# Output projection of a linear-attention block: the order of 1/den loads, x rows, first FFN weights and PQ products

## Chip, cores and metric

One core of a Trainium2 chip runs the whole kernel in one launch. The metric is the device time in microseconds (us), the median over several runs; lower is better. The kernel before takes 782.52 us (three runs, 782.25 to 782.95).

## What is computed

An adaLN-conditioned transformer block over 2048 tokens of width 1024: linear attention with 32 heads of width 32, then a GEGLU feed-forward network (FFN) of width 3584. All inputs are bf16.

```python
mod = (silu(c) @ w_mod)                 # six rows of 1024: sa, ca, ga, sb, cb, gb
h = layernorm(x) * (1 + ca) + sa
q, k, v = split(h @ wqkv)               # 32 heads
pq, pk = phi(q), phi(k)                 # where(t > 0, t + 1, exp(t)) + 1e-6
kv = einsum('bhsd,bhse->bhde', pk, v);  z = sum_s pk
num = pq @ kv;  den = pq . z + 1e-6
x = x + ga * ((num / den) @ wo)
h = layernorm(x) * (1 + cb) + sb
x = x + gb * ((gelu(h @ w_gate) * (h @ w_up)) @ w_down)
```

## The kernel before

The tokens are cut into 16 chunks of 128, and the chunks into 4 groups of 512 (`sg` 0 to 3), each group into two halves of 256 tokens (`h` 0 and 1). Five instruction streams run side by side, one for each engine: PE (TensorE), DVE (VectorE), ACT (ScalarE), POOL (GpSimd) and SP, which issues nearly all DMAs. Every operation is recorded by `sch.op` or `sch.dma` with the bytes it reads and writes; `Sched` works out the semaphore waits from them. Within one engine, work runs in the order of its stream. SP has eight semaphore lanes in turn, so each DMA also waits for the landing of the eighth one before it (`Sched.LANES`, `dma`).

The order of the streams: PE's and SP's are those of the program text. DVE, ACT and POOL are put in a new order by `sch.reorder` from the K/Q stage up to the point `mark[1]`, just before the projection's loop over chunks 3 to 13; there a planner with costs and due times picks the next ready operation. `deps=` adds an order by hand: an operation with it waits for the one named. Behind `mark[1]` DVE's order is again that of the text, so what stands in the table `SLOT` comes in the order written.

The stages around the change:

- **M and KV.** `m_tile(g, k, ...)` makes M = pk^T x for eight blocks `g` of 128 head columns, three column tiles `k` each: 24 tiles, in the list `tiles`, with matmuls at L895. ACT copies each tile to the buffer `mb` (L900). When a block is done, `m_t(g)` transposes it by a DMA from `mb` to `mtb` (L703); "mT7" below is that of the last block. `kv_prod(g, ...)` (L913) multiplies it by the V weights, and DVE masks the result into `kvt` (L920). `w2_pair(i)` (L1201) multiplies two blocks of `kvt` by the output weights to W2, which ACT or DVE copies from PSUM (L1208).
- **1/den.** `den(pr_, b)` computes the denominators of two groups (L1240), DVE takes the reciprocal (L1245, L1246), and a DMA stores it in DRAM (L1248). `rb_load(sg, hs)` loads it back for one half of a group, spread over the partitions: four DMAs of 256 KB for each half (L1260). There are two buffers, `RB[0]` for even groups and `RB[1]` for odd ones.
- **PQ products.** `pq_scale(sg, h, gs)` multiplies pq in place by 1/den on DVE (L1273), four operations for each half of a group.
- **Projection.** `wo_mm(c, b0, gs)` accumulates pq @ W2 for chunk `c` in PSUM banks `b0` and `b0 + 1` (L1283); after the last block DVE adds x and the row sum (L1291, "x1"). Chunks 0 to 2 are interleaved with the last KV and W2 products; chunks 3 to 13 follow whole, with `SLOT[c]()` behind each; chunks 14 and 15 stand within the first FFN unit. The banks go round, so chunk 4 needs those of chunk 0.
- **LN2 and FFN.** For each chunk POOL and ACT compute the second layernorm (L664 to L679, L674, L660), and a DMA transposes the rows (`h2a`, `h2b`, L703). `x_dma(c0, c1)` loads rows of x again (L592); chunks 7 and up had been overwritten before. `wt_dma(u)` loads the gate and up weights of FFN unit `u` (two DMAs of 512 KB, L1371); DVE and ACT form sums of them for the products (`t_sum`, L1433).

The table `HOOK` says what stands behind which of the 24 M tiles. Its end, before:

```python
19: "kv4", 20: "den1 ps0.0", 21: "gbr", 22: "ps0.1", 23: "rb2.0"}
```

Here `rb2.0` is `rb_load(2, (0,))` and `ps0.1` is `pq_scale(0, 1, ...)`. In the loop over tiles, `m_t(g)` of tile 23 comes ahead of the hooks of tile 23, so mT7 stands on SP ahead of `rb2.0`.

Of the kernel before, what the change touches and what calls it, by code (L numbers as in the profile page):

```python
# [7 lines left out]
ACTF = mybir.ActivationFunctionType  # L8
# [322 lines left out]
def bass_adaLN_cond__linear_attn_block__geglu_ffn__prompt_kernel(  # L331
# [18 lines left out]
    with ExitStack() as es:  # L350
# [150 lines left out]
        def r_wt(i, t0=0, t1=2, k0=0, k1=NDC):  # L501
            return [(OFF_WS + i * 8192 + t * 4096 + k0 * 512, OFF_WS + i * 8192 + t * 4096 + k1 * 512, f"wt{i}") for t in range(t0, t1)]
# [28 lines left out]
        def r_rb(i, h, g0=0, g1=NG):  # L531
            return [(OFF_RB[i] + (h * NG + g0) * 1024, OFF_RB[i] + (h * NG + g1) * 1024, f"rb{i}")]
# [58 lines left out]
        def x_dma(c0, c1):  # L591
            return sch.dma(Q, lambda e: e.dma_start(XALL[:, c0:c1, :], x_v[:, c0:c1, :]), wr=r_xs(c0, c1), note=f"x{c0}")  # L592
# [312 lines left out]
        def m_t(g):  # L905
            i = g % 2
            tdma(Q, MTB[i][:, :, :], MB[g][:, :], r_mb(g), r_mtb(i), f"mT{g}")

        def kv_prod(g, bank):
            i = g % 2  # L910
            o = None
            for dc in range(NDC):
                o = sch.op(T, lambda e, dc=dc: e.matmul(PS(bank, 0, P), WV[:, g, dc, :], MTB[i][:, dc, :],  # L913
                                                        start=(dc == 0), stop=(dc == NDC - 1)),
                           rd=r_wv(g) + r_mtb(i), pwr=(pr(bank) if dc == 0 else ()), note=f"kv g{g} dc{dc}")
            pset_writer(bank, o)
            z = 64 * (g % 2)
            for h in range(2):
                a, gz = 64 * h, g // 2 * 2 + h
                sch.op(V, lambda e, a=a, gz=gz: e.tensor_tensor(KVT[z:z + 64, gz, 0:64], ps_all[a:a + 64, bank * 512 + a:bank * 512 + a + 64], BMASK[a:a + 64, a:a + 64], ALU.mult),  # L920
                       prd=pr(bank), rd=r_sm("bmask"), wr=r_kvt(gz, gz + 1), note=f"kvt{g}", overwrite_ok=True)

        bank_i = [0, 4]
# [268 lines left out]
        def z32():  # L1192
            sch.op(V, lambda e: e.tensor_tensor(Z32[:], BM32[:], ZCOLS[:, :].unsqueeze(2).to_broadcast([P, NG, NH]), ALU.mult),
                   rd=r_sm("bm32") + r_sm("zcols"), wr=r_sm("z32"), note="z32")

        def w2_pair(i, b0=4):
            for hf in range(2):
                for r in range(2):
                    for h in range(2):
                        b, g = b0 + 2 * r + hf, 2 * i + h  # L1200
                        sch.op(T, lambda e, b=b, g=g, h=h, r=r, hf=hf: e.matmul(ps_all[64 * h:64 * h + 64, b * 512:(b + 1) * 512], KVT[64 * r:64 * r + 64, g, 0:64],  # L1201
                               WO[64 * r:64 * r + 64, g, hf * 512:(hf + 1) * 512], start=True, stop=True),
                               rd=r_kvt(g, g + 1) + r_wo(g, hf * 512, (hf + 1) * 512), pwr=pr(b), note=f"w2 {i}.{hf}", overwrite_ok=True)
            for r in range(2):
                b, g = b0 + 2 * r, 2 * i + r
                w_, p_ = W2[:, g, :], ps_all[:, b * 512:(b + 2) * 512]
                eng = V if i > 1 and r else A
                sch.op(eng, lambda e, w_=w_, p_=p_, eng=eng: e.activation(w_, p_, ACTF.Copy) if eng == A else e.tensor_copy(w_, p_),  # L1208
                       prd=pr(b) + pr(b + 1), wr=r_w(OFF_WK, "w2", g), note=f"w2cp{g}")

        def wofold(kc):
# [53 lines left out]

        GH = [((0, 2), (2, 4)), ((4, 6), (6, 8))]

        def pq_scale(sg, h, gs):
            i, t0 = sg % 2, h * HW
            for g0, g1 in gs:  # L1270
                ap = PQ[sg][:, g0:g1, t0:t0 + HW]
                rng = r_pq(sg, g0, g1, t0, t0 + HW)
                sch.op(V, lambda e, ap=ap, i=i, h=h, g0=g0, g1=g1: e.tensor_tensor(ap, ap, RB[i][:, h, g0:g1, :], ALU.mult),  # L1273
                       rd=rng + r_rb(i, h, g0, g1), wr=rng, deps=rb_ops[sg, h], note=f"pqs{sg}.{h}.{g0}")

        x1_ops, s_ops = {}, {}

        def wo_mm(c_, b0, gs):
            sg, ci = divmod(c_, CPG)
            last = [None, None]  # L1280
            for g in gs:
                for half in range(2):
                    last[half] = sch.op(T, lambda e, g=g, half=half: e.matmul(  # L1283
                        PS(b0 + half), PQ[sg][:, g, ci * P:(ci + 1) * P], W2[:, g, half * 512:(half + 1) * 512],
                        start=(g == 0), stop=(g == NG - 1)),
                        rd=r_pq(sg, g, g + 1, ci * P, (ci + 1) * P) + r_w(OFF_WK, "w2", g, half * 512, (half + 1) * 512),
                        pwr=(pr(b0 + half) if g == 0 else ()), note=f"wo c{c_} g{g} h{half}")
            if gs[-1] == NG - 1:
                for half in range(2):
                    pset_writer(b0 + half, last[half])  # L1290
                x1_ops[c_] = sch.op(V, lambda e: e.scalar_tensor_tensor(XALL[:, c_, :], ps_all[:, b0 * 512:(b0 + 2) * 512], 1.0, XALL[:, c_, :],  # L1291
                                                           op0=ALU.mult, op1=ALU.add, accum_out=STA[:, c_, 0:1]),
                       prd=pr(b0) + pr(b0 + 1), rd=r_x(c_), wr=r_x(c_) + r_smc("st", c_, 48),
                       deps=[s_ops[0, 0, 1]] if c_ == 13 else [], note=f"x1 c{c_}")
                if c_ < 2 * CPG:
                    ln_nmean(c_)

# [2 lines left out]
        NWO = 5  # L1300
        tiles = [(g, k) for g in range(4) for k in range(3)] + [(g, 0) for g in range(4, NG)] + [(g, k) for g in range(4, NG) for k in (1, 2)]
        HOOK = {0: "ga", 6: "kv0", 10: "kv1", 11: "w0", 13: "kv2", 15: "modp kv3 z32", 16: "den0", 17: "w1 rb0.0 rb0.1", 18: "",
                19: "kv4", 20: "den1 ps0.0", 21: "gbr", 22: "ps0.1", 23: "rb2.0"}
        st = {}

        def hook_run(f):
            if f[:2] == "kv":
                kv_prod(int(f[2:]), 4)
            elif f == "ga":
                ga_pass()  # L1310
            elif f == "gbr":
                assert mdone[0] == 64
                gb_rows()
            elif f == "modp":
                mod_pass()
            elif f == "z32":
                z32()
            elif f[:3] == "den":
                st[int(f[3:])] = den(int(f[3:]), 5)
                st[int(f[3:])]()  # L1320
            elif f[:2] == "ps":
                pq_scale(int(f[2]), int(f[4]), GH[0] + GH[1])
            elif f[:2] == "rb":
                rb_load(int(f[2]), (int(f[4]),))
            elif f[0] == "w":
                w2_pair(int(f[1:]))

        for n, (g, k) in enumerate(tiles):
            m_tile(g, k, n % 4, n % 2)
            if n == len(tiles) - 1:  # L1330
                kv_prod(5, 4)
            if k == 2:
                m_t(g)
            if n == NWO:
                wo_load(2)
                wo_load(3)
            for _ in range(3):
                mod_step()
            if 2 <= n <= 9:
                wofold(n - 2)  # L1340
            while pend and n > 1:
                wm_dma(*pend.pop(0))
            if n in (6, 7):
                gb_load(0, n - 6)
            if n == 11:
                gb_load(1, 0)
                gb_load(1, 1)
            for f in HOOK.get(n, "").split():
                hook_run(f)
        wo_mm(0, 0, [0, 1, 2, 3])  # L1350
        w2_pair(2)
        wo_mm(1, 2, [0, 1, 2])
# [2 lines left out]
        wo_mm(0, 0, [4, 5])  # L1355
        rb_load(1)
        rb_load(2, (1,))
        w2_pair(3)
        wo_mm(1, 2, [3, 4, 5])
        wo_mm(2, 4, list(range(6)))  # L1360
        for c_ in range(3):
            wo_mm(c_, 2 * c_, [6, 7])

        def wd_dma(q):
            f0, f1 = 4 * q, 4 * q + 4
            sch.dma(Q, lambda e: e.dma_start(WDT[q][:], wd_v[:, f0:f1, :]), wr=[t_ for fc in range(f0, f1) for t_ in r_wd(fc)], note=f"wd{q}")

        def wt_dma(u):
            i, f0 = u % 2, u % NFP * 256
            for t, v_ in enumerate((wg_v, wu_v)):  # L1370
                sch.dma(Q, lambda e, t=t, v_=v_: e.dma_start(WT[i][:, t, :, :], v_[:, :, f0:f0 + 256]), wr=r_wt(i, t, t + 1), note=f"wt{t} u{u}")  # L1371

        def wo_chunk(c_, b0):
            wo_mm(c_, b0, list(range(NG)))
# [220 lines left out]
            if last:  # L1595
                pset_writer(b, o)

        pq_scale(2, 0, GH[0] + GH[1])

        def r_wh(q, r, cc, name, j0, j1):  # L1600
            return [(WDQ[q] + (2 * j + r) * 2048 + cc * 1024, WDQ[q] + (2 * j + r) * 2048 + (cc + 1) * 1024, name) for j in range(j0, j1)]
# [164 lines left out]
        def cb1():  # L1766
            sch.op(V, lambda e: e.tensor_scalar(CB1T[:, :], CBT[:, :], 1.0, None, op0=ALU.add), rd=r_sm("cbT"), wr=r_sm("cb1T"))

        SLOT = {2: lambda: (pq_scale(1, 0, GH[0] + GH[1]), x_dma(NXR, 10)),
                3: lambda: pq_scale(1, 1, GH[0] + GH[1]),  # L1770
                4: lambda: (cb1(), wt_dma(0)),
                5: lambda: (pq_scale(2, 1, GH[0] + GH[1]), rb_load(3, (0,))),
                6: lambda: (mod2(0, 0, 2), x_dma(10, 12)),
                7: lambda: (t_sum(0, 0), t_sum(0, 1), mod2(0, 2, 2), x_dma(12, 14)),
# [210 lines left out]
```

## Time and profile before

| | |
|---|---|
| median of the timed runs | 782.52 us (782.25 to 782.95) |
| profiled execution, first to last instruction (span) | 780.9 us, 1.6 less than the median |
| PE busy | 770.2 us, 99% |
| DVE busy | 645.9 us, 83% |
| ACT busy | 374.6 us, 48% |
| POOL busy | 47.5 us, 6% |
| DMA moved | 130.22 MB, mean 167 GB/s |
| M matmuls (L895), share of the chain that ended last | 7.2% |
| projection matmuls (L1283), share of the same chain | 7.1% |

The profile gives no other time of the profiled execution than its span; what lies around it, the start and the end, is taken as the 1.6 us to the median. A profile row has the engine, the line, what is written and read, and a duration. "idle before <- releaser" tells how long the engine stood still and whose work ended that. The chain is followed back from the last instruction, at each step to what released it. For a DMA the row on SP is the issue alone; when the data has landed is told apart, as us from issue to landing.

### The profile page before, as it was taken

What the parts mean: (1) busy time and instruction counts of PE and PEld (TensorE: products, weight loads), DVE (VectorE), ACT (ScalarE), POOL (GpSimd) and SP (SyncE); (2) the same over time, 40 slices, a digit from 0 to 9 for tenths busy, and PEclk for the clock granted to TensorE, in tenths of its full rate; (3) what the DMA queues carried; (4) which work ended last, traced back from release to release, by engine and by line L of the source; (5) the groups of instructions that cost most, each with busy time, mean ns of one, the idle gap of its engine ahead of it and who ended that gap; (6) DMA issues with size and microseconds to landing.
All of it is one profiled execution on the core that took longest, in us unless ns stands there. A gap on an engine that the chain in (4) does not pass through costs nothing.

```text
span 780.9 us, 10753 instructions
## 1 busy us (share of the span) xinstructions
PE 770.2 (99%) x3825; PEld 496.2 (64%) x3883; DVE 645.9 (83%) x964; ACT 374.6 (48%) x629; POOL 47.5 (6%) x126
## 2 busy tenths in 40 slices
PE   8999999999999999999999999999999999999998
PEld 4444445666445667667676767667676576677766
DVE  6699988897899878787989888888989888676767
ACT  2497743242466487878755555555555211111111
POOL 2031300000321011100000000000000000000000
PEclk9999999999999999999999999999999999999999
DMA  9879749939999358867353865535356334443331
GB/s 284 256 167 252 158 91 215 255 80 196 203 287 231 82 138 212 230 175 215 99 145 108 250 211 172 148 96 161 97 147 221 111 127 139 144 141 114 126 125 60
DMA packets 196940, 130.22 MB, mean 167 GB/s; under 512 B 69516, under 2 KB 182420, under 8 KB 195864
## 3 DMA queue, kind: packets, MB, share of 16 engines
q1 hardware_dynamic: 196872, 129.55, 62.4%
q8 instruction: 30, 0.49, 0.3%
q14 instruction: 22, 0.18, 0.1%
q10 hardware_dynamic: 16, 0.00, 0.0%
HBM read 92.55 MB, written 23.35 MB: 148 GB/s over the span
## 4 chain that ended last, share of the span: by engine, by line
PE 95%; SPq 2%; DMA 1%; DVE 1%; issue 1%; ACT 0%; DVEq 0%; ACTq 0%
PE ps_all L1458 45%; PE ps_all L1672 21%; PE ps_all L895 7%; PE ps_all L934 7%; PE ps_all L1283 7%; PE ps_all L880 5%; PE ps_all L1593 1%; SPq L598 1%; DMA wmq<-in_w_mod_dram 1%; SPq L603 1%; DMA h1T<-xh 0%; PE ps_all L913 0%; PE ps_all L1201 0%; PE ps_all L1240 0%; DVE h1T L724 0%
## 5 line engine op out<-in xcount | busy, mean ns | idle before, releaser
L1458 PE MATMUL ps_all<-ss,tp 128*128 128x512 f32 x896 | 214.3, 396 | 0.0
L1458 PEld LDWEIGHTS ps_all<-ss,tp 128*128 128x128 f32 x896 | 168.3, 188 | 37.8 <-DVE ss L1413 0.2
L1672 PE MATMUL ps_all<-dt,sb 128*128 128x512 f32 x424 | 102.5, 398 | 0.0
L1481 ACT ACTIVATE ge<-ps_all 128x512 f32<-128x512 f32 x112 | 64.1, 597 | 73.8 <-DVE ps_all L1469 62.1
L1458 PE MATMUL ps_all<-h2a,wt 128*128 128x512 bf16 x421 | 95.7, 379 | 1.8
L1672 PEld LDWEIGHTS ps_all<-dt,sb 128*128 128x128 f32 x424 | 79.6, 188 | 18.5 <-DVE sb L1648 0.3
L1476 DVE TENSOR_TENSOR ps_all<-ps_all,es 128x512 f32<-128x512 f32 x54 | 37.6, 699 | 49.4 <-ACT es L1466 49.0
L1488 DVE TENSOR_TENSOR ys<-ge,ps_all 128x512 bf16<-128x512 f32 x112 | 74.4, 684 | 3.8 <-PE ps_all L1672 0.5
L1458 PEld LDWEIGHTS ps_all<-h2a,wt 128*128 128x128 bf16 x448 | 38.0, 98 | 57.3 <-ACT ps_all L1463 16.9
L1433 DVE TENSOR_TENSOR tp<-wt 128x1024 fp32r<-128x1024 bf16 x56 | 68.1, 1217 | 1.8 <-DMA wt<-in_B_w_up_dram 1.8
L1433 DVE TENSOR_TENSOR tp<-wt,tp 128x1024 fp32r<-128x1024 bf16 x56 | 68.2, 1218 | 0.0
L934 PE MATMUL ps_all<-h1T,wq 128*128 128x512 bf16 x256 | 56.7, 379 | 0.0
L880 PE MATMUL ps_all<-wk,h1T 128*128 128x512 bf16 x239 | 55.3, 379 | 1.1 <-DMA wk<-in_A_wqkv_dram 0.5
L1283 PE MATMUL ps_all<-w,pq 128*128 128x512 bf16 x249 | 55.7, 379 | 0.5 <-issue 0.2
L1458 PE MATMUL ps_all<-ar,tp 128*128 128x512 f32 x224 | 55.5, 390 | 0.0
L869 ACT ACTIVATE eb<-ps_all 128x512 f32<-128x512 f32 x64 | 36.3, 594 | 37.6 <-PE ps_all L880 16.0
L1672 PE MATMUL ps_all<-wd,ya 128*128 128x512 bf16 x199 | 47.5, 380 | 0.7
L1458 PEld LDWEIGHTS ps_all<-ar,tp 128*128 128x128 f32 x224 | 42.1, 188 | 8.9
L1463 ACT ACTIVATE ps_all<-ps_all 128x512 f32<-128x512 f32 x56 | 32.6, 582 | 26.8 <-PE ps_all L1458 26.5
L934 PEld LDWEIGHTS ps_all<-h1T,wq 128*128 128x128 bf16 x256 | 25.0, 98 | 30.0
L1283 PEld LDWEIGHTS ps_all<-w,pq 128*128 128x128 bf16 x256 | 24.6, 98 | 30.3 <-issue 1.1
L1643 ACT ACTIVATE sb<-ya 128x896 fp32r<-128x896 bf16 (+1 forms) x16 | 14.5, 913 | 58.8 <-PE ps_all L1672 58.8
(141 smaller groups left out, 976.3 us busy)
## 6 DMA issues: line engine op xcount, KB each, us to landing
wt<-in_B_w_gate_dram SPq DMA_DIRECT2D x28, 512.0 KB, 4.0
wt<-in_B_w_up_dram SPq DMA_DIRECT2D x28, 512.0 KB, 5.2
scr_y<-ys SPq DMA_DIRECT2D x28, 512.0 KB, 3.2
ya<-scr_y SPq DMA_DIRECT2D x14, 896.0 KB, 4.9
rb<-scr_rd SPq DMA_DIRECT2D x32, 256.0 KB, 6.0
wd<-in_B_w_down_dram SPq DMA_DIRECT2D x7, 1024.0 KB, 7.6
wmst<-in_w_mod_dram SPq DMA_DIRECT2D x6, 1024.0 KB, 6.2
wmq<-in_w_mod_dram SPq DMA_DIRECT2D x8, 512.0 KB, 7.5
```

Of the source, the lines that this page charges most:

```text
L869: sch.op(A, lambda e: e.activation(EB[i][:, :], PS(bank), ACTF.Exp), prd=pr(bank), wr=rng, note=f"{note}.exp")
L880: o = sch.op(T, lambda e, dc=dc: e.matmul(PS(bank), H1[sg][:, ci, dc, :], W_[:, dc, jg * 512:(jg + 1) * 512], start=(dc == 0), stop=(dc == ...
L895: o = sch.op(T, lambda e, c_=c_: e.matmul(PS(bank, 0, n), PK[c_][:, g * P:(g + 1) * P], xrow(c_, o_, o_ + n), start=(c_ == 0), stop=(c_ == ...
L934: o = sch.op(T, lambda e, dc=dc: e.matmul(PS(b), WQ[:, dc, qc * P:(qc + 1) * P], H1[sg][:, :, dc, :], start=(dc == 0), stop=(dc == NDC - 1 ...
L1283: last[half] = sch.op(T, lambda e, g=g, half=half: e.matmul(PS(b0 + half), PQ[sg][:, g, ci * P:(ci + 1) * P], W2[:, g, half * 512:(half + ...
L1433: sch.op(V, lambda e: e.tensor_tensor(TP[k][:], in0, in1 if k in (0, 2) else in1[:], ALU.subtract), rd=r0 + r1, wr=r_tp(k), deps=[x1_ops[7 ...
L1458: o = sch.op(T, lambda e, l_=l_, r_=r_, dc=dc: e.matmul(PS(b), l_, r_, start=fresh and dc == 0, stop=dc == ND2 - 1, skip_group_check=True) ...
L1463: sch.op(A, lambda e: e.activation(PS(BB + t), PS(BA + t), ACTF.Copy), prd=pr(BA + t), pwr=pr(BB + t), note="pcp")
L1476: sch.op(V, lambda e: e.tensor_tensor(PS(BC + t), PS(BC + t), ES[t][:, :], ALU.add), prd=pr(BC + t), rd=r_2k(OFF_ES[t], f"es{t}"), pwr=pr( ...
L1481: sch.op(A, lambda e: e.activation(GE[i][:, :], PS(b), ACTF.Gelu_apprx_tanh), prd=pr(b), wr=r_2k(OFF_GE[i], f"ge{i}"), note="gelu")
L1488: sch.op(V, lambda e: e.tensor_tensor(YS[s_][:, 2 * h:2 * h + 2, t, :], q(GE[i][:, :]), q(PS(b + 1)), ALU.mult), rd=r_2k(OFF_GE[i], f"ge{i ...
L1672: o = sch.op(T, lambda e, l_=l_, r_=r_, j=j, dst=dst: e.matmul(dst, l_[:, 0, :], r_, start=(k in (1, 5) or own is not None) and j == js[0] ...
```

## The change

Five edits, all of them of order:

1. `rb2.0` (four loads of 256 KB, group 2's first half) moves from `HOOK[23]` to `HOOK[22]`, so it stands on SP ahead of mT7.
2. `x_dma(NXR, 10)` (chunks 7 to 9, 768 KB) and `wt_dma(0)` move from slots 2 and 4 of the projection to right behind `rb_load(2, (1,))`, ahead of the first four LN2 transposes on SP. `wt_dma` is defined earlier in the text for that.
3. `pq_scale(1, 0, ...)` moves from slot 2 to before `wo_mm` of chunks 0 to 2 is finished; x1 of chunk 0 gets `deps` on its four operations, and x1 of chunks 1 and 2 on the one before.
4. The first two products of group 2's first half get `deps`: one on the last `kvt`, the other on the last copy of W2.
5. The other two move from the same place to slot 4, behind x1 of chunk 4.

DVE's stream from the last `kvt` on was: W2 copy, three products of group 2, x1 of chunks 0 to 2, one product of group 2, four of group 1, x1 of chunk 3. It becomes: product of group 2, W2 copy, product of group 2, four of group 1, x1 of chunks 0 to 3. PE's, ACT's and POOL's streams stay as they are. The diff, without the definitions that only move:

```diff
@@ kv_prod
+                kvt_op[0] = sch.op(V, ..., note=f"kvt{g}", overwrite_ok=True)
@@ w2_pair
+                w2_op[0] = sch.op(eng, ..., note=f"w2cp{g}")
@@ pq_scale
+                o = sch.op(V, ..., deps=rb_ops[sg, h] + after.get((sg, h, g0), []), note=f"pqs{sg}.{h}.{g0}")
+                ops.append(o)
+            return ops
@@ wo_mm
-                       deps=[s_ops[0, 0, 1]] if c_ == 13 else [], note=f"x1 c{c_}")
+                       deps=[s_ops[0, 0, 1]] if c_ == 13 else o_pq if c_ == 0 else [x1_ops[c_ - 1]] if c_ < 3 else [], note=f"x1 c{c_}")
@@ HOOK
-                19: "kv4", 20: "den1 ps0.0", 21: "gbr", 22: "ps0.1", 23: "rb2.0"}
+                19: "kv4", 20: "den1 ps0.0", 21: "gbr", 22: "ps0.1 rb2.0"}
@@ behind the M tiles
         wo_mm(0, 0, [4, 5])
         rb_load(1)
         rb_load(2, (1,))
+        x_dma(NXR, 10)
+        wt_dma(0)
         w2_pair(3)
         wo_mm(1, 2, [3, 4, 5])
         wo_mm(2, 4, list(range(6)))
+        o_pq = pq_scale(1, 0, GH[0] + GH[1])
         for c_ in range(3):
             wo_mm(c_, 2 * c_, [6, 7])
...
-        pq_scale(2, 0, GH[0] + GH[1])
+        after.update({(2, 0, 0): kvt_op[:], (2, 0, 2): w2_op[:]})
+        pq_scale(2, 0, GH[0])
...
-        SLOT = {2: lambda: (pq_scale(1, 0, GH[0] + GH[1]), x_dma(NXR, 10)),
+        SLOT = {2: lambda: None,
                 3: lambda: pq_scale(1, 1, GH[0] + GH[1]),
-                4: lambda: (cb1(), wt_dma(0)),
+                4: lambda: (cb1(), after.update({(2, 0, 4): [x1_ops[4]], (2, 0, 6): [x1_ops[4]]}), pq_scale(2, 0, GH[1])),
```

More of the change, by code (lines that the diff above doesn't have):

```diff
@@ L907, in m_t @@
             tdma(Q, MTB[i][:, :, :], MB[g][:, :], r_mb(g), r_mtb(i), f"mT{g}")
+        kvt_op = [None]
         def kv_prod(g, bank):
@@ L919, in kv_prod @@
                 a, gz = 64 * h, g // 2 * 2 + h
-                sch.op(V, lambda e, a=a, gz=gz: e.tensor_tensor(KVT[z:z + 64, gz, 0:64], ps_all[a:a + 64, bank * 512 + a:bank * 512 + a + 64], BMASK[a:a + 64, a:a + 64], ALU.mult),
+                kvt_op[0] = sch.op(V, lambda e, a=a, gz=gz: e.tensor_tensor(KVT[z:z + 64, gz, 0:64], ps_all[a:a + 64, bank * 512 + a:bank * 512 + a + 64], BMASK[a:a + 64, a:a + 64], ALU.mult),
                        prd=pr(bank), rd=r_sm("bmask"), wr=r_kvt(gz, gz + 1), note=f"kvt{g}", overwrite_ok=True)
@@ L1194, in z32 @@
                    rd=r_sm("bm32") + r_sm("zcols"), wr=r_sm("z32"), note="z32")
+        w2_op = [None]
         def w2_pair(i, b0=4):
@@ L1207, in w2_pair @@
                 eng = V if i > 1 and r else A
-                sch.op(eng, lambda e, w_=w_, p_=p_, eng=eng: e.activation(w_, p_, ACTF.Copy) if eng == A else e.tensor_copy(w_, p_),
+                w2_op[0] = sch.op(eng, lambda e, w_=w_, p_=p_, eng=eng: e.activation(w_, p_, ACTF.Copy) if eng == A else e.tensor_copy(w_, p_),
                        prd=pr(b) + pr(b + 1), wr=r_w(OFF_WK, "w2", g), note=f"w2cp{g}")
@@ L1266, in bass_adaLN_cond__linear_attn_block__geglu_ffn__prompt_kernel @@
         GH = [((0, 2), (2, 4)), ((4, 6), (6, 8))]
+        after = {}
         def pq_scale(sg, h, gs):
-            i, t0 = sg % 2, h * HW
+            i, t0, ops = sg % 2, h * HW, []
             for g0, g1 in gs:
@@ L1272, in pq_scale @@
                 rng = r_pq(sg, g0, g1, t0, t0 + HW)
-                sch.op(V, lambda e, ap=ap, i=i, h=h, g0=g0, g1=g1: e.tensor_tensor(ap, ap, RB[i][:, h, g0:g1, :], ALU.mult),
-                       rd=rng + r_rb(i, h, g0, g1), wr=rng, deps=rb_ops[sg, h], note=f"pqs{sg}.{h}.{g0}")
+                o = sch.op(V, lambda e, ap=ap, i=i, h=h, g0=g0, g1=g1: e.tensor_tensor(ap, ap, RB[i][:, h, g0:g1, :], ALU.mult),
+                           rd=rng + r_rb(i, h, g0, g1), wr=rng, deps=rb_ops[sg, h] + after.get((sg, h, g0), []), note=f"pqs{sg}.{h}.{g0}")
+                ops.append(o)
+            return ops
         x1_ops, s_ops = {}, {}
@@ L1349, in bass_adaLN_cond__linear_attn_block__geglu_ffn__prompt_kernel, with wt_dma @@
                 hook_run(f)
+        def wt_dma(u):
+            i, f0 = u % 2, u % NFP * 256
+            for t, v_ in enumerate((wg_v, wu_v)):
+                sch.dma(Q, lambda e, t=t, v_=v_: e.dma_start(WT[i][:, t, :, :], v_[:, :, f0:f0 + 256]), wr=r_wt(i, t, t + 1), note=f"wt{t} u{u}")
         wo_mm(0, 0, [0, 1, 2, 3])
@@ L1366, in wd_dma @@
             sch.dma(Q, lambda e: e.dma_start(WDT[q][:], wd_v[:, f0:f1, :]), wr=[t_ for fc in range(f0, f1) for t_ in r_wd(fc)], note=f"wd{q}")
[L1368 to L1371, printed above, removed]
         def wo_chunk(c_, b0):
```

## Prediction

> **What bounds the kernel now.** I read four views of the profile: the page, the chain of waits around the changed place, the queue that issues the transfers, and the landing times of single transfers. The page comes first.
>
> ```profile
> PE 770.2 (99%) x3825; PEld 496.2 (64%) x3883; DVE 645.9 (83%) x964; ACT 374.6 (48%) x629; POOL 47.5 (6%) x126
> PE 95%; SPq 2%; DMA 1%; DVE 1%; issue 1%; ACT 0%; DVEq 0%; ACTq 0%
> ```
>
> TensorE (PE) is busy for 770.2 of 780.9 us and makes up 95% of the chain that ended last. So an edit pays only where it removes PE idle time, and costs only where it adds some. The chain from 190 to 200 us holds the end of M and the start of the output projection:
>
> ```profile
> 190.62 0.46 ACT mb L900
> ...
> 194.71 0.92 PE ps_all L913 x16
> ...
> 197.05 0.16 issue
> ```
>
> The row at 194.71 is kv_prod(6) and kv_prod(7), eight matmuls each, so PE comes to kv_prod(7) at 194.71 + 0.46 = 195.17. That product reads what M's last transpose, mT7, writes. The PE waits here are 0.46 + 0.16 = 0.62 us, and from 197.21 to 241.62 there are none: 206 matmuls in 44.41 us are 0.2156 us each, one after the other. Next the issues on SP:
>
> ```profile
> 176.69 3.76 SPq L1260 DMA_DIRECT2D rb<-scr_rd  x8
> 180.55 1.23 SPq L703 DMA_TRANSPOSE mtb<-mb  x1
> 185.74 0.35 SPq L1248 DMA_DIRECT2D scr_rd<-rdc  x1
> ...
> 188.45 0.56 SPq L849 DMA_DIRECT2D scr_row<-mrg  x1
> 191.15 1.26 SPq L703 DMA_TRANSPOSE mtb<-mb  x1
> 192.51 2.84 SPq L1260 DMA_DIRECT2D rb<-scr_rd  x6
> ```
>
> In turn these are: eight 1/den loads with transpose mT5 right behind them, the store of the second 1/den, and, at 191.15, mT7 with the third group's loads behind it. The last view is the landing times; its last column is us from issue to landing. Each line is of one issue alone: the first and the last of those eight loads, mT5, the store, mT7.
>
> ```profile
> rb<-scr_rd SPq DMA_DIRECT2D x1, 256.0 KB, 3.6
> rb<-scr_rd SPq DMA_DIRECT2D x1, 256.0 KB, 8.6
> mtb<-mb SPq DMA_TRANSPOSE x1, 9.0
> scr_rd<-rdc SPq DMA_DIRECT2D x1, 128.0 KB, 5.3
> mtb<-mb SPq DMA_TRANSPOSE x1, 3.1
> ```
>
> The reader is to see one line of transfers served in turn. The first of eight loads lands at 176.69 + 3.6 = 180.3 and the last (issued at 180.03) at 188.6, so each takes (188.6 - 180.3) / 7 = 1.19 us. mT5 was issued behind them and took 9.0 us, to 189.55: 0.9 us after the last load. mT7, with nothing queued ahead of it, took 3.1 us, to 194.25, 0.9 us before PE wants it.
>
> **The third group's first loads ahead of mT7.** Four loads of 256 KB (1 MB) go in front of mT7 on SP. They may not start before the store has landed: 185.74 + 5.3 = 191.04. They also wait for VectorE (DVE) to finish with the buffer, where the row that starts at 185.58 ends at 188.01, which is earlier. SP is free from 188.45 + 0.56 = 189.01, so it waits until about 191.1, just where it waited for ScalarE's copy of M before (191.15). Six loads were issued in 2.84 us, 0.47 each, so four hold SP for 1.9 us and mT7 is issued at 193.0, not 191.15. Behind SP's wait stand only mT7 and later loads.
>
> The landing follows from the line. The first load lands at 191.1 + 3.6 = 194.7, the fourth 3 x 1.19 later at 198.3, and mT7 0.9 after that at 199.2. PE came to kv_prod(7) at 195.17, so it stands idle for 4.0 us; with some 0.1 for the hop from landing to start (mT7 was issued 0.07 after ScalarE's copy ended at 191.08) I take **+4.1 us**. PE takes its work in order, so the 206 matmuls of the projection stand behind this wait. Bounds: if mT7 were not held up by the loads at all it would land at 193.0 + 3.1 = 196.1, 0.95 us of idle time; if transfers were each 10% slower, 4.6. I take the queue value since the mT5 row is the same pair of transfers in the same order.
>
> [...]
>
> **What that brings the other engines.** DVE had idled for these loads and for the first gate/up weights:
>
> ```profile
> 199.83 1.89 DVE L1273 TENSOR_TENSOR pq<-pq,rb 128x512 bf16<-128x512 bf16 x3 [1.45 <-DMA rb<-scr_rd]
> 224.04 1.23 DVE L1433 TENSOR_TENSOR tp<-wt 128x1024 fp32r<-128x1024 bf16 x1 [1.80 <-DMA wt<-in_B_w_up_dram]
> ```
>
> Both waits go or shrink. Neither stands on the chain (no PE wait between 197.21 and 241.62), so I give 0 for them; at most the 0.16 at 197.05 could come back.
>
> **The x rows and first weights behind the last 1/den load.** 768 KB and 2 x 512 KB leave before the LN2 transposes instead of among them. With the line above, the second group's eight loads and the third group's last four land by 199.2 + 12 x 1.19 = 213.5. The x rows take 2.0 us behind a transpose (issued at 211.15, landed at 218.0, where the first h2a transpose landed at 209.87 + 6.1 = 216.0), the weights 1.84 each (up landed at 218.43 + 5.4 = 223.8, gate at 222.0): line empty at 219.2, and the first h2a transpose lands near 220.1. That is 4.1 later than before, just the shift of the whole stage, since before it stood behind 1/den loads too. On SP each DMA waits for the eighth before it: the x rows for the load that lands near 205, the weights for the next two, so SP is through by 209 and holds up no transpose (the first is ready at 209.87 + 4.1). Cost 0; the cover is that the projection runs until 241.62 + 4.1.
>
> **The PQ products by hand order.** No instruction is added; eight of the multiplies (2.50 us for four, 0.62 each) stand in another order. The first product of group 2 now stands ahead of the copy of W2's last block: its load lands at 198.3 and the kvt rows end about 200.3, so it costs that copy 0.6 us, and the copy (1.23 us, behind w2_pair(3), which ends near 201.1) is done by 202.4, where the first matmul on it comes at 201.5 + 4.1 = 205.6. The x1 sums of chunks 0 to 2 now wait for group 1's four products: its loads land at 199.2 + 4 x 1.19 = 204.0, four products take 2.5, x1 of chunk 0 takes 1.23, done at 207.7. Chunk 4, which needs its banks and the products, comes 46 matmuls after 197.21, at 207.1, now 211.2: margin 3.5 us. If that cover failed, each us of lateness would be a us of PE idle. The last two products of group 2's first half go behind x1 of chunk 4, done near 218, for chunk 8, which comes 64 matmuls after chunk 4 (13.8 us), at 225.0. All 0.
>
> **Sum.** The profiled span of 780.9 becomes 785.0. The median of the timed runs, 782.52, lies 1.6 above the span (start and end around it, untouched): 782.52 + 4.1 = **786.6 us**.
>
> **Rivals.** *The clock falls in the gap.* 4.1 us is longer than any PE gap that this trace has inside (0.62 us) or at its end:
>
> ```profile
> 778.00:780.90 2.90, 0.00 (x0) 0.00 (x0) 0.72 (x2) 0.00 (x0) 0.00 (x0) 1.00 0.27 90
> 2.28 4.43 PE L949 MATMUL ps_all<-warm 128*128 128x512 bf16 x11
> ```
>
> The first row is the stretch after the last matmul: 2.90 us without PE work, granted clock (last but two) still 1.00; that column reads 1.00 at the cold start too, so matmul durations tell more. The second, from PE's timeline, is the price of a cold start: 11 matmuls in 4.43 us, where the warm 0.2156 each make 2.37, so up to 2.1 us lost. Part of a cold spell can lie inside the gap: +1 to +2.1, 787.6 to 788.7. For it: 4.1 exceeds 2.9. Against: no row shows a fall. [...] Chance 0.27.
>
> *The transpose isn't held up (not slower by the bound below).* mT7 lands 3.1 after its issue: 0.95 us idle, 783.5. It decides if mT7 lands before 195.17 + 1.5 = 196.7. Against it: mT5's 9.0 us, and 6.1 us for the h2b transpose issued behind four loads at 224.35. Chance 0.12.
>
> *The loads' edit does nothing to PE and the small waits close.* If the store landed earlier than 191 and the loads were past before mT7, the 0.16 and part of the 0.46 come back: 781.9. Against: the store's 5.3 us precedes every edit. Chance 0.05.
>
> **How the numbers follow.** Forecast 0.56, clock 0.27, not held up 0.12, small gain 0.05. The range takes in the first two, with 0.7 us below 4.1 for the landing and the runs' scatter and 0.3 above the cold clock's upper end: 785.4 to 789.0, leaving out 0.17. About 0.2% (1.6 us) is what a measurement can tell from no change. Slower by more: 0.83. Within: both small cases, 0.15. Faster needs 1.6 us of PE idle to vanish where 0.62 exists: 0.02.
>
> **What would show it.** Right: a PE wait of about 4 us at kv_prod(7) (L915 in the changed kernel) released by the mtb transfer; that transfer issued near 193.0 with 6 us or more to land; DVE's 1.45 and 1.80 waits gone; chunks 3 to 13 without PE waits. Wrong: mT7 landing in about 3 us, a PE wait at chunk 4 (x1 of chunk 0 late), or a wait in the first FFN products. A matmul mean near 0.4 us just after the gap would be the clock.

## Result and the profile after

| | before | after |
|---|---|---|
| median of six runs each | 782.51 us (782.13 to 783.62) | 787.65 us (785.73 to 788.72) |
| span of the profiled execution | 780.9 us | 785.9 us (in a run of 787.72 us) |

The ratio is 1.0062 [1.0051, 1.0073]: slower by about 5.1 us. The shares of the chain that ended last, from the page of the changed kernel:

```profile
PE 94%; DMA 2%; SPq 2%; DVE 0%; issue 0%; DVEq 0%
```

DMA has taken one point of the chain from PE. The chain of waits, from where the second 1/den is stored (start, us, what):

```profile
185.84 4.68 DMA scr_rd<-rdc
...
190.54 0.32 SPq L1264
...
192.35 6.01 DMA mtb<-mb
198.36 0.14 issue
198.50 0.73 PE ps_all L915 x8
199.23 1.71 PE ps_all L1291 x4
```

Where the chain before ran through ScalarE's copy of M and PE, it now runs store, four issues (the first is shown), mT7, kv_prod(7) (L915). The landings of single transfers (last column: us from issue to landing): the store, the first and the fourth of the four loads, issued at 190.54 and 191.83, and mT7, issued at 192.35:

```profile
scr_rd<-rdc SPq DMA_DIRECT2D x1, 128.0 KB, 4.7
rb<-scr_rd SPq DMA_DIRECT2D x1, 256.0 KB, 3.4
rb<-scr_rd SPq DMA_DIRECT2D x1, 256.0 KB, 5.6
mtb<-mb SPq DMA_TRANSPOSE x1, 6.0
```

The loads land from 193.93 to 197.45, 1.17 us apart, and mT7 at 198.36, 0.9 behind the last. PE's timeline (start, us, line, tiles, count, idle time before):

```profile
194.67 0.61 PE L915 MATMUL ps_all<-mtb,wv 128*128 128x128 bf16 x8
198.50 0.73 PE L915 MATMUL ps_all<-mtb,wv 128*128 128x128 bf16 x8 [3.22 <-DMA mtb<-mb]
```

PE stands still for 3.22 us. Behind that, four matmuls of 128x512 take 1.71 us in the chain, 0.43 each, twice the 0.2156 of before. The granted clock says why. This is busy time by stretch, for the gap, the 3.8 us behind it and the next 10; the last three columns are granted clock, DMA share and GB/s:

```profile
195.28:198.40 3.12, 0.00 (x0) 0.00 (x0) 0.45 (x2) 0.00 (x0) 0.00 (x0) 1.00 1.17 223
198.40:202.20 3.80, 3.70 (x21) 1.33 (x22) 1.30 (x4) 0.23 (x1) 0.00 (x0) 0.56 1.00 207
202.20:212.20 10.00, 10.00 (x48) 4.50 (x47) 7.88 (x13) 3.27 (x5) 1.39 (x5) 1.00 1.01 211
```

The clock is half for 3.41 us (198.84 to 202.25). From the first matmul of M to the first of the FFN, before took 241.62 - 114.05 = 127.57 us and after 4.97 more: 3.3 is kv_prod(7)'s later start (198.50 for 195.17), and the rest, about 1.7, is half of the 3.41 us. That is the whole of 785.9 - 780.9. DVE's waits from 188 to 246 us have neither the loads nor the weights among them any more (us in total, times, longest):

```profile
DVE xall L1299 <- PE ps_all L1291: 5.0, 4, 2.2
DVE kvt L922 <- PE ps_all L915: 4.6, 3, 3.5
```

The 1.45 and 1.80 us went, and DVE now waits for PE instead (the third and last row of that view, 3.3 us, is for PE too).

### The profile page after: what moved, and what is told of

Same layout as the page of the kernel before. It is cut to its first block, busy times and chain, and to the rows that moved or that the text cites. A ratio compares the mean times of both kernels' runs of the same rounds, so it can differ in the third digit from the quotient of the medians.

```text
span 785.9 us, 10814 instructions
## 1 busy us (share of the span) xinstructions
PE 776.0 (99%) x3883; PEld 497.0 (63%) x3883; DVE 646.2 (82%) x964; ACT 374.5 (48%) x629; POOL 48.4 (6%) x126
## 4 chain that ended last, share of the span: by engine, by line
PE 94%; DMA 2%; SPq 2%; DVE 0%; issue 0%; DVEq 0%
PE ps_all L1469 45%; PE ps_all L1684 21%; PE ps_all L936 7%; PE ps_all L1291 7%; PE ps_all L895 6%; PE ps_all L880 6%; PE ps_all L1604 1%; SPq L598 1%; DMA wmq<-in_w_mod_dram 1%; DMA mtb<-mb 1%; SPq L603 1%; DMA scr_rd<-rdc 1%; PE ps_all L915 0%; PE ps_all L1205 0%; PE ps_all L1244 0%; SPq L592 0%
## 5 line engine op out<-in xcount | busy, mean ns | idle before, releaser
L1469 PE MATMUL ps_all<-h2a,wt 128*128 128x512 bf16 x448 | 101.5, 380 | 0.0
L1291 PE MATMUL ps_all<-w,pq 128*128 128x512 bf16 x256 | 57.5, 384 | 0.0
```

Source lines behind the costliest of these rows:

```text
L1291: last[half] = sch.op(T, lambda e, g=g, half=half: e.matmul(PS(b0 + half), PQ[sg][:, g, ci * P:(ci + 1) * P], W2[:, g, half * 512:(half + ...
L1469: o = sch.op(T, lambda e, l_=l_, r_=r_, dc=dc: e.matmul(PS(b), l_, r_, start=fresh and dc == 0, stop=dc == ND2 - 1, skip_group_check=True) ...
```

## Experiments

My theory was: edit 1 alone costs the time, by PE's idle time at kv_prod(7) and by the half clock that follows it; the other edits cost nothing. The rivals: the other edits cost part of it, or the loads slow something else. The kernel before, run beside them in three sets, had medians of 782.73, 782.84 and 782.53; each ratio below is to the kernel before of its own set.

**Edit 1 alone, on the kernel before**

```diff
-  21: "gbr", 22: "ps0.1", 23: "rb2.0"}
+  21: "gbr", 22: "ps0.1 rb2.0"}
```

> The kernel before with edit 1 alone. If the queue ahead of mT7 is the cause: a PE wait of 3.3 us at kv_prod(7) and a spell at half clock worth 1.7 us behind it, so 787.5 us. If the other edits carry the cost: within 0.5 us of 782.5, and mT7's landing is hidden.

Measured: 787.55 us, ratio 1.0062 [1.005, 1.0075]. PE's waits from 188 to 262 us:

```profile
PE ps_all L913 <- DMA mtb<-mb: 3.5, 1, 3.5
```

The one edit makes the whole difference, with nearly the same wait (3.5 us for 3.2) and nearly the same time at half clock (3.4 us, from 198.6 to 202.0). PE's only other wait there is one of 0.3 us.

**Edit 1 undone, the others kept**

```diff
-  21: "gbr", 22: "ps0.1 rb2.0"}
+  21: "gbr", 22: "ps0.1", 23: "rb2.0"}
```

> The changed kernel with edit 1 taken back (the four loads behind mT7 again), edits 2 to 5 kept. If the queue ahead of mT7 is the cause: mT7 lands within about 3.1 us of its issue, no PE wait at kv_prod(7), granted clock 1.000. One new wait is expected to come out that the gap had covered: group 1's loads land near 204.6 as in the kernel before, four products end near 207.1, x1 of chunk 0 near 208.3, where chunk 4 wants its banks at 207.1, so a PE wait of about 1.2 us there: 783.7 us. If edits 2 to 5 carried the cost instead: above 786, with the waits where they were in the changed kernel.

Measured: 785.12 us, ratio 1.003 [1.0019, 1.0042], clock 1.00 in all six runs. kv_prod(7) doesn't wait for mT7 (its matmuls follow those of kv_prod(6) in one row, 16 in 1.05 us from 194.89), but 2.4 us over before remain, 1.4 above the expected 783.7. PE's timeline has a wait in the middle of the projection:

```profile
197.52 9.88 PE L1291 MATMUL ps_all<-w,pq 128*128 128x512 bf16 x45 [0.16 <-issue]
209.26 2.98 PE L1291 MATMUL ps_all<-w,pq 128*128 128x512 bf16 x12 [1.86 <-DVE xall L1299]
```

and DVE's shows what made x1 of chunk 0 late, group 1's loads:

```profile
205.44 2.50 DVE L1279 TENSOR_TENSOR pq<-pq,rb 128x512 bf16<-128x512 bf16 x4 [3.81 <-DMA rb<-scr_rd]
207.97 1.22 DVE L1299 SCALAR_TENSOR_TENSOR xall<-ps_all,xall 128x1024 bf16<-128x1024 f32 x1
```

The wait is 1.9 us where 1.2 was expected, and PE's rows show 0.4 us more lost in the first FFN unit, for which the expectation had nothing. Edit 3 costs nothing in the changed kernel, where PE comes 5 us later to chunk 4; here it costs that wait. The next four runs take the hidden prices apart.

**Edit 3 alone, on the kernel before**

```diff
+        o_pq = pq_scale(1, 0, GH[0] + GH[1])
         for c_ in range(3):
             wo_mm(c_, 2 * c_, [6, 7])
-  deps=[s_ops[0, 0, 1]] if c_ == 13 else []
+  deps=[s_ops[0, 0, 1]] if c_ == 13 else o_pq if c_ == 0 else [x1_ops[c_ - 1]] if c_ < 3 else []
-  SLOT = {2: lambda: (pq_scale(1, 0, GH[0] + GH[1]), x_dma(NXR, 10)),
+  SLOT = {2: lambda: x_dma(NXR, 10),
```

> The kernel before with the third edit alone: group 1's four products ahead of x1 of chunk 0, and chunks 1 and 2 chained behind it; all transfers in their old places. Theory: mT7 lands in about 3 us and PE reaches chunk 4 near 207.1, but group 1's loads land near 205.3, so x1 of chunk 0 is done near 209: a PE wait of 1.5 to 2.0 us at chunk 4, released by x1, and nothing in the first FFN unit: 784.2 to 784.8. Rival (only the early x rows and weights delay things): 782.5 to 782.9.

Measured: 785.66 us, ratio 1.0035 [1.0023, 1.0047]. PE's waits:

```profile
PE ps_all L1285 <- DVE xall L1293: 1.8, 1, 1.8
PE ps_all L1461 <- DVE ss L1416: 0.3, 1, 0.3
```

The wait is the one expected; the time is 0.9 above the expected range. The span grew by 783.6 - 780.9 = 2.7, of which the two waits are 2.1. PE's timeline places the rest: it is 0.2 late at kv_prod(5) already (190.63 for 190.42), 2.2 late at the first FFN matmul (243.63 for 241.45) and 2.75 late where the `ar` products of the first FFN unit begin (262.08 for 259.33). So 2.0 us are lost at chunk 4 and 0.6 in the first FFN unit, without edit 2.

**Edit 2 alone, on the kernel before**

```diff
         rb_load(2, (1,))
+        x_dma(NXR, 10)
+        wt_dma(0)
         w2_pair(3)
...
-  SLOT = {2: lambda: (pq_scale(1, 0, GH[0] + GH[1]), x_dma(NXR, 10)),
+  SLOT = {2: lambda: pq_scale(1, 0, GH[0] + GH[1]),
-          4: lambda: (cb1(), wt_dma(0)),
+          4: lambda: cb1(),
```

> The kernel before with edit 2 alone. The prediction gave it no cost, with the shift of the whole stage as its cover; here nothing is shifted. If that cover was needed: the h2a transposes land near 221.5 instead of 216, DVE's and ACT's second layernorm run late, and PE waits 0.5 to 2 us in the first FFN unit: 783.0 to 784.5 us. If it costs nothing without cover too: 782.5 us, with DVE's 1.8 us wait for the first up weights gone.

Measured: 785.1 us, ratio 1.0027 [1.0016, 1.0037], 0.6 above the expected range. The first LN2 transpose lands at 222.17 instead of 216.0, behind 1.75 MB of x rows and weights. DVE idles for the transpose, so its x1 sums and its sums for the first FFN unit come late, and PE waits there:

```profile
223.15 2.13 DVE L724 TENSOR_SCALAR h2a<-h2a,cb1T,sbT 128x256 bf16<-128x256 bf16 x8 [3.88 <-DMA h2a<-xl]
```

```profile
PE ps_all L1460 <- DVE xall L1291: 1.2, 2, 0.7
PE ps_all L1460 <- DVE ss L1415: 0.5, 2, 0.3
```

**Edits 2, 4 and 5 without 1 and 3's dependencies** (the run with edit 1 undone, less the `deps` of x1)

```diff
-  deps=[s_ops[0, 0, 1]] if c_ == 13 else o_pq if c_ == 0 else [x1_ops[c_ - 1]] if c_ < 3 else []
+  deps=[s_ops[0, 0, 1]] if c_ == 13 else []
```

> The kernel with edit 1 taken back (785.12 us) and without the two deps on x1 of edit 3, so x1 of chunks 0 to 2 again stands ahead of group 1's products on DVE; edits 2, 4 and 5 stay. If the 1.86 us wait at chunk 4 is the price of edit 3: that wait is gone and the time falls by about 2 us, less what edit 2 then shows (the first h2a transpose lands some 5 us later than in the kernel before, so waits of 0.2 to 1.5 us in the first FFN unit): 783 to 784.5 us. If the wait came from late loads and not from the order: 785 us as before.

Measured: 785.26 us, ratio 1.0025 [1.0016, 1.0035]. The wait at chunk 4 is gone, yet the time is that of the run with it (785.12), above the range expected for this case: edit 2's waits of 0.7 and 0.4 us in the first FFN unit stand in its place. The rival had that number (785), but by a wait at chunk 4 that would stay. Edit 2 alone gives 785.1, so edits 4 and 5 add nothing that shows; and the prices of 2 and 3 do not add up, since a wait at chunk 4 gives edit 2's transposes their cover (with that wait, in the run with edit 1 undone, the FFN waits are 0.2 us instead of 1.1).

**Edit 2 undone, the others kept**

```diff
         rb_load(2, (1,))
-        x_dma(NXR, 10)
-        wt_dma(0)
...
-  SLOT = {2: lambda: None,
+  SLOT = {2: lambda: x_dma(NXR, 10),
-          4: lambda: (cb1(), ..., pq_scale(2, 0, GH[1])),
+          4: lambda: (cb1(), ..., pq_scale(2, 0, GH[1]), wt_dma(0)),
```

> The changed kernel with the second edit undone: x rows and the first weights issued in slots 2 and 4 as before, all other edits kept. Theory (the early x rows and weights cost nothing as long as the gap at kv_prod(7) has pushed the whole projection back by 5 us): the same wait of 3.2 us and the same half-clock spell, no wait in the first FFN unit, 787.3 to 787.9. Rival (they cost something there too): 785.5 to 787.0.

Measured: 787.83 us, ratio 1.0066 [1.0053, 1.0079], a wait of 3.4 us at kv_prod(7), and no wait over 0.2 us in the first FFN unit. In the changed kernel edit 2 costs and brings nothing.

**Two, and three, of the four loads ahead of mT7**, the rest behind it (three: 3 for 2)

```diff
-  22: "ps0.1 rb2.0"}
+  22: "ps0.1 ra2.0", 23: "rz2.0"}
+  elif f[:2] == "ra": rb_load(2, (0,), range(2))
+  elif f[:2] == "rz": rb_load(2, (0,), range(2, HPG))
```

> The changed kernel with two of the four loads ahead of mT7 and two behind it. If mT7 stands in one line with the loads: it lands 2 x 1.19 = 2.4 us earlier than in the changed kernel, near 196.0, the PE wait is 0.9 us, too short for the clock to fall, 783.4 us. If any load ahead of mT7 brings the whole cost (a fixed price of the change of order): 787.6 us. If the price is SP's issue time alone (0.47 us for each load): a wait of about 0.2 us at most, 782.6 us.

> The changed kernel with three of the four loads ahead of mT7. One line of transfers: mT7 lands one load (1.2 us) earlier than in the changed kernel, so the PE wait is about 2.2 us. What it tells of the clock: if a gap must be near 3 us or more for the fall, no run falls and the time is about 785.5 us (2.2 more than the kernel before, and some tenths for waits in the first FFN unit); if 2.2 us are enough, the granted clock is 0.998 in most runs and the time 787.

Measured: two 784.49 us, ratio 1.0025 [1.0015, 1.0034]; three 784.72 us, 1.0026 [1.0016, 1.0036]. PE's first wait in each:

```profile
PE ps_all L915 <- DMA mtb<-mb: 1.1, 1, 1.1
```

```profile
PE ps_all L915 <- DMA mtb<-mb: 2.2, 1, 2.2
```

Waits of 1.1, 2.2 and (four loads) 3.2 to 3.5 us: each load ahead of mT7 added 1.0 to 1.3 us to the wait (in the changed kernel the loads land 1.17 us apart). The time with two is 1.1 above the expected 783.4, that with three 0.8 below the nearer of its two expected times. The times of two and three differ less than the waits, since with two a wait of 0.3 us is left in the first FFN unit and with three none. With three, the mean clock was 0.998 in two of nine runs, the two that took 786.2.

**Twelve extra matmuls in the gap** (their product is thrown away)

```diff
         kv_prod(6, 4)
+        for _ in range(12):
+            sch.op(T, lambda e: e.matmul(PS(7), PQ[0][:, 0, 0:P], W2[:, 0, 0:512], start=True, stop=True), ...)
         kv_prod(7, 5)
```

> The changed kernel with twelve more 128x512 matmuls between kv_prod(6) and kv_prod(7), on data that is there (12 x 0.2156 = 2.6 us of PE work in the gap, written to a bank that nobody reads). If half of the clock in the us behind the gap is a part of the loss: the wait shrinks to about 0.7 us, the granted clock is 1.000 in every run and the time is 787.65 - 1.7 = 785.9 us. If the clock has no part in it: 787.6 us as without the twelve.

Measured: 785.92 us, ratio 1.0045 [1.0031, 1.0059]; clock 1.00 in four of five runs, 0.999 in one. PE's timeline:

```profile
194.77 2.75 PE L1368 MATMUL ps_all<-w,pq 128*128 128x512 bf16 x12
197.98 0.61 PE L915 MATMUL ps_all<-mtb,wv 128*128 128x128 bf16 x8 [0.46 <-DMA mtb<-mb]
```

kv_prod(7) comes when it did, to 0.2 us (3.66 us behind the start of kv_prod(6), 3.83 in the changed kernel), so what is saved is nearly all the clock: 787.65 - 785.92 = 1.7 us, as read from the trace, or 1.95 if each is counted from the kernel before of its own set. The 785.92, 3.2 above its own kernel before, is what the gap costs with the clock held.

**The same gap filled with work of the projection**

```diff
         kv_prod(6, 4)
-        kv_prod(7, 5)
         wo_mm(0, 0, [4, 5])
+        wo_mm(1, 2, [3, 4, 5])
+        kv_prod(7, 5)
...
         w2_pair(3)
-        wo_mm(1, 2, [3, 4, 5])
```

> The changed kernel, with ten matmuls of the projection (0.2156 us each, 2.16 in all) moved from behind kv_prod(7) to ahead of it. Theory (the price is PE's idle time at kv_prod(7) and the spell at half clock that a gap of 3.2 us starts): the wait shrinks from 3.2 to about 1.1 us, the clock does not fall, kv_prod(7) starts at the same time as in the changed kernel; w2_pair(3) now comes right behind it and waits 0.3 to 0.8 us for the kvt rows. With the stage 2 us earlier, the cover of the early x rows and weights is thinner, as with two loads ahead (784.5): waits of 0.3 to 1 us in the first FFN unit. 784.3 to 785.3. Rival (the loads slow something else, and the idle time is not the cause): the time stays at 787.6.

Measured: 787.36 us, ratio 1.0063 [1.005, 1.0076], a miss of 2 us. PE's timeline:

```profile
195.72 2.32 PE L1291 MATMUL ps_all<-w,pq 128*128 128x512 bf16 x10
199.67 0.61 PE L915 MATMUL ps_all<-mtb,wv 128*128 128x128 bf16 x8 [1.63 <-DMA mtb<-mb]
200.66 0.88 PE L1205 MATMUL ps_all<-wo,kvt 64*64 64x512 bf16 x8 [0.38 <-DVE kvt L922]
202.88 0.38 PE L1291 MATMUL ps_all<-w,pq 128*128 128x512 bf16 x1 [1.34 <-ACT w L1212]
```

The wait at kv_prod(7) shrank, but the ten matmuls had been the cover of what comes behind it: the mask to `kvt`, W2's last product and its copy. PE now waits for these, 1.63 + 0.38 + 1.34 = 3.35 us in all. The number is the rival's, the rows are not: it isn't the idle time at kv_prod(7) that is the price but the whole chain from mT7 to the copy of W2, of which PE has only some 22 independent matmuls to hide. Against the one wait of 0.16 us before, that is 3.2 of the 785.2 - 780.9 = 4.3 us by which the span grew; 0.7 more had come up before kv_prod(6) (195.28 for 194.57 in PE's timeline), and some 0.4 is not placed. Two of the six runs, the profiled one among them, had clock 1.00, the four others 0.996 or 0.997, so in most runs the clock fell too, though no single wait in the trace is longer than 1.63 us; where it fell, no trace shows.

**mT7 on ScalarE's DMA queue**, past the loads on SP

```diff
-  tdma(Q, MTB[i][:, :, :], MB[g][:, :], ...)
+  tdma(A if g == NG - 1 else Q, MTB[i][:, :, :], MB[g][:, :], ...)
```

> The changed kernel with mT7 issued from ACT's DMA queue instead of SP's, behind mT6's landing. If the line is that of SP's queue alone: mT7 lands 3 to 4 us after its issue near 192, the PE wait at kv_prod(7) is under 1 us; then group 1's loads, which land near 203.5, make x1 of chunk 0 late for chunk 4 by some tenths, so 783.5 to 784.5 us, clock 1.000. If both queues stand in one line before the same DMA engines: mT7 lands near 198.4 as in the changed kernel, 787.6 us.

Measured: 793.96 us, ratio 1.0139 [1.0125, 1.0153], outside both expectations. The landing of mT7, issued at 190.93, and PE's wait:

```profile
mtb<-mb ACTq DMA_TRANSPOSE x1, 12.9
```

```profile
PE ps_all L915 <- DMA mtb<-mb: 9.2, 1, 9.2
```

The clock was half for about 10.2 us, from 199.0, in the midst of that wait, to 209.2. A queue of its own was no way past the loads here: the transpose, issued beside them, took 12.9 us, and 6.0 behind them in the changed kernel.

## Why the prediction came out as it did

The mechanism and its place were right: the new order on SP's queue, PE's wait at kv_prod(7) released by the mtb transfer, both DVE waits gone, no wait at chunk 4 or in the FFN. 787.65 lies in the range, but it is the time of the rival in which the clock falls (787.6 to 788.7, chance 0.27), not of the forecast (786.6). That the forecast came within 1.1 us of it is in part luck: two errors, 0.9 us too much idle time and 1.7 us of half clock left out, have opposite signs.

- **The idle time was 4.1 in the sum and is 3.2.** The store took 4.7 us, not 5.3, so everything began 0.5 earlier (190.52 for 191.04). The first load took 3.4 for 3.6 and the loads stood 1.17 apart for 1.19: the last landed at 197.45, not 198.3. The 0.9 us from there to mT7 held, and PE came 0.1 later. With the clock held, the sum would have been 785.7; the filled gap measured 785.92.
- **"Clock held" as the likeliest case is the step that failed.** The chance of 0.27 for the fall was my estimate: no row of the trace before shows what a gap of that length inside the span does. The fall came in 14 of the 16 runs with a gap of 3.2 to 3.5 us (five of six after, four of five with edit 1 alone, five of five with edit 2 undone; mean clock 0.997 or 0.998 in each). The prediction also took the 2.90 us without PE work at the end of the trace, at a clock of 1.00, as a sign that a gap of that length does no harm; in that trace the clock falls to 0.50 at 780.96, 3.0 us behind the end of the last matmul (777.94) and 0.02 us past the span.
- **The price of the fall** was bounded by 1 to 2.1 and is 1.7 in the trace and between the runs.
- **Queue order or not.** The rival "not held up" (783.5) is dead: mT7 took 6.0 us. In each of the traces before and after, the 286 transfers on SP's queue whose landing is on record landed in the order of their issue, and the waits of 1.1, 2.2 and 3.2 us for two, three and four loads are those of transfers served in turn.
- **Edits 2 and 3 at nothing.** Right for this kernel (edit 1 alone 787.55, all but edit 2 787.83, all 787.65), and by the cover that was named, the shift of the stage. But the price without the cover wasn't given: 2.3 us for edit 2 (785.1 - 782.84) and 3.1 for edit 3 (785.66 - 782.53). For edit 3 the "margin 3.5 us" was less than the forecast delay of 4.1, so it rested on that delay wholly: without the gap, x1 of chunk 0 is 1.8 us late.
- **The DVE waits at nothing.** Right: 3.25 us less waiting for loads and weights brought PE nothing.
- **Two slips that changed little.** The 0.46 us in the prediction's "0.62 us" of PE waits is a stretch in which the chain runs through ScalarE's copy; in PE's timeline the matmuls of kv_prod(5) fill it (190.42 to 191.03), and PE's one listed wait from 188 to 262 us is the 0.16. The rival that small waits close had 0.2 us to win, not 0.6. And the lower end of the range, 785.4, lies 1.2 us below the forecast, not the 0.7 that the text gives.

No version that was run beats the kernel before: each edit that was tried alone (1, 2, 3) costs 2 to 5 us, and 4 and 5 showed no effect. A version with 4 and 5 alone was not run.

## What to carry to other kernels

Ahead of a move on a DMA queue, ask which transfer on it PE waits for soonest, and with how much slack: mT7 had 0.9 us, and the loads of 256 KB put before it landed 1.17 us apart. A wait of an engine that is off the chain is no reason to give its loads a place before that transfer. A cost of nothing that rests on the delay from another edit of the same change should be priced without that delay as well, and a PE gap like those of 3.2 to 3.5 us here should be priced with the half clock too (the clock fell in 14 of 16 runs, worth 1.7 us in the trace), one of 2.2 us with a part of it (it fell in two of nine runs).

## What was not expected of the hardware

The clock fell at different places of the gap: 0.3 us behind its end in the changed kernel (at 198.84, gap of 3.22 us) and with edit 1 alone (at 198.6, gap of 3.54 us), 2.6 us into it with edit 2 undone (at 197.7, gap of 3.4 us), and 4.3 us into it with mT7 on ScalarE's queue (at 199.0, gap of 9.21 us). In the last it stayed at half for about 10.2 us, against 3.41 in the changed kernel. With edit 2 undone it is at half again from 784.74 on, at the end of the trace (behind the length of the stretch stands PE's busy time; the granted clock is third from the end):

```profile
781.33:784.74 3.41, 1.22 (x6) 0.68 (x4) 1.89 (x3) 0.00 (x0) 0.00 (x0) 1.00 0.23 77
784.74:785.56 0.82, 0.00 (x0) 0.00 (x0) 0.00 (x0) 0.00 (x0) 0.00 (x0) 0.50 0.00 0
```

In the 3.41 us before that fall PE worked for 1.22 us and was idle for 2.2, as far as the ends of matmuls, which the profile models, can be trusted. A gap of 2.2 us, with three loads ahead, had a mean clock of 0.998 in two of nine runs and no fall in the profiled one; one of 1.86 us, with edit 1 undone, had 1.00 in all six. What sets the moment of the fall, no run shows.

The DMA transpose mT7 took 3.1 us with no load ahead of it (the kernel before) and 6.0 behind four loads on one queue (the changed kernel); on another queue beside them it took 12.9. The loads suffered as well: the third of the four, issued at about 190.9, took 6.2 us to land, for 4.95 in the changed kernel. Why the two queues slowed each other, no run shows.
